# Retention and two feed-forward layers: layer 2's second product by seven products in two of its three pairs

## The chip, the cores and the metric

The kernel runs on one core of one Trainium2 chip. The metric is the device time in microseconds (us) of one execution: 847.47 us is the median of three runs of the kernel before (847.09 to 847.84). The engines named below are PE (TensorE, with its weight loads shown as PEld), DVE (VectorE), ACT (ScalarE), POOL (GpSimd) and SP (SyncE, which issues nearly all DMAs).

## The reference

```python
def _attn_ref(q, k, v):                      # batch 4, heads 8, sequence 576, head size 64
    scores = scale * np.matmul(q, k.transpose(0, 1, 3, 2))
    gamma = 1.0 - 2.0 ** (-5.0 - np.arange(H))
    Dmat = np.where(rel >= 0, gamma[:, None, None] ** rel[None, :, :], 0.0)
    return np.matmul(scores * Dmat[None], v)
...
x = attn_out.transpose(0, 2, 1, 3).reshape(2304, 512)
h = x @ moe_w_in;  g = np.maximum(0.01 * h, h);            x = g @ moe_w_out     # 512 -> 2048 -> 512
h = x @ moe2_w_in; g = h * (1.0 / (1.0 + np.exp(-h)));     return g @ moe2_w_out # 512 -> 2048 -> 512
```

The retention (attention without a softmax) feeds two feed-forward layers of the same size over 2304 tokens. Each layer has a first product (512 to 2048), a nonlinearity, and a second product (2048 to 512). Weights arrive as 64-bit floats and are turned into 32-bit floats on the chip.

## The kernel before

Every number that PE multiplies is split into a high and a low part (a `float32r` copy made by ACT in line 116, and the rest made by DVE in line 117). Each product is three matmuls: high by high, high by low, low by high (`PASSES`).

**The front** covers the first 1536 tokens of layer 1: three blocks of 512 tokens, 16 tiles of the hidden size (`f`) each, 48 *steps* in all (the loop of line 779). A step does `gemm1` (12 matmuls, `h<-xs,wi`), the nonlinearity and its split (`activate`), the splits of a weight tile (`split_wi`, `split_wo`), and `gemm2` of the step two before (12 matmuls, `acc<-g,wo`). The retention of the later tokens is laid between these matmuls at the times of `ATT_AT`. A layer 1 tile is *decoded* from 64-bit to 32-bit (`decode`, lines 371 to 393: two ACT and four DVE operations for 128x1024 numbers) in steps 0 to 13. The first 32 steps (`FIXED`) stand in a written order on every engine; the last 16 are ordered by a scheduler.

**The pairs.** Then come four *pairs* of 2x384 tokens: pair 0 is the rest of layer 1, pairs 1 to 3 are layer 2. A pair has eight *quads* (`k`), each two tiles of the hidden size. In a quad the first product is computed by seven products of sub-matrices in place of eight (`quad`; `sums_x` and `sums_w` make the sums of inputs and weights that this needs): 7x6 = 42 matmuls of 128x384 (`a` and `b`). Results are added in SBUF by DVE (line 594), go through the nonlinearity, and are split (`finish`) into `gh` and `gl`. The second product (`outputs`) is the plain one: 36 matmuls of 128x512 for a quad of pairs 1 to 3 (`outputs_y`), into six banks of PSUM that stay open over the pair (`acc0`, `acc1`, `att`). PE runs the second product of a quad between the seven products of the next one (`left`), which gives ACT and DVE time.

Layer 2's tiles are decoded in pairs 0 and 1 (`decoded`, line 866). Pair 1 also writes the split sums and the split second weights to DRAM (`kept`); pairs 2 and 3 fetch them (`fetch`, and line 527 in `weights_out`). PE and SP follow the written order in the pairs; ACT and DVE are ordered by the scheduler.

Of the kernel before, what the change touches and what calls it, by code (L numbers as in the profile page):

```python
# [26 lines left out]

FIXED = 2 * NF
TILE = 384
# [10 lines left out]

ATT_AT = (3.2, 8.4, 8.4, 13.8, 14, 22, 22, 29.8, 29.8, 36.5, 36.5, 43.1)
ATT = [(u, ATT_AT[2 * i], ATT_AT[2 * i + 1]) for i, u in enumerate(UNITS[2:])]
# [21 lines left out]
def retention_mlp_kernel(ctx: ExitStack, tc: tile.TileContext, qkva, qkvb, w1, w2, consts, out):  # L64
# [11 lines left out]
    x_p = pool("x", 1)  # L76
    s_p = pool("s", 29)
    hs_p = pool("hs", 2)
# [3 lines left out]
    st_p = pool("st", 4, stack=heads, side=right)  # L82
    acc_p = pool("acc", 1, PSUM)
    att_p = pool("att", 1, PSUM)
    ps_p = pool("ps", 2, PSUM)

    def slot(shape, dt, name):
        return s_p.tile(shape, dt, tag="s", name=name)

    cst = const.tile([128, NC + NP * CH], F32, name="cst")  # L90
# [256 lines left out]
    def load_w(layer, f, parts=(0, 1)):  # L347

        if (layer, f) not in w64:
            wraw[layer, f] = slot([128, 1024], F32, "wraw")  # L350
            w64[layer, f] = dec_p.tile([128, 1024, 2], I32, tag="w64", name="w64")
        src = (w1, w2)[layer][f].bitcast(I32)
        for i in parts:
            nc.sync.dma_start(out=w64[layer, f][:, i * 512:(i + 1) * 512].rearrange("p n t -> p (n t)"),
                              in_=src[:, i * 1024:(i + 1) * 1024])
        if len(parts) == 2:
            wdec.append((wraw[layer, f], w64[layer, f]))

    def half(f, i, by_act):

        c = slice(i * 512, (i + 1) * 512)
        return decode(wraw[0, f][:, c], w64[0, f][:, c], by_act)
# [44 lines left out]
    def split_x(layer, i, c, half=None, engine=nc.vector):  # L407
        p0, n = BLOCKS[i]
        if not half:
            xs[layer, i, c] = slot([128, 2, 512], F32R, "xs")  # L410
# [18 lines left out]
    def activate(layer, i, f):  # L429

        n = BLOCKS[i][1]
        h = hidden.pop((layer, i, f))
        hs = hs_p.tile([128, 512], F32, tag="hs", name="hs")
        g = slot([128, 2, 512], F32R, "g")
# [69 lines left out]

    dram = pool("scratch", 1, bass.MemoryType.DRAM)
    kept = {k: dram.tile([128, 22, 256], F32, tag=f"kept{k}", name="kept") for k in range(NF // 2)}
    PARTS = (("ha", 0, 3), ("la", 3, 3), ("hs", 6, 4), ("ls", 10, 4))

    def weights(p, k):

        t = {n: slot([128, m, 256], F32R, n) for n, _, m in PARTS}
        ha, la, hs, ls = t.values()
        for i, name in enumerate(("a11", "a12", "a22")):
            ww[p, k, name] = ha[:, i], la[:, i]
        for i in range(4):
            ww[p, k, f"s{i + 1}"] = hs[:, i], ls[:, i]
        return t

    def weights_out(p, k):

        for i in range(2):
            f = 2 * k + i
            wsp[p, f] = w = slot([128, 2, 512], F32R, "wo")
            there = kept[k][:, 14 + 4 * i:18 + 4 * i]
            here = w.bitcast(F32).rearrange("p a (b n) -> p (a b) n", b=2)
            if p > 1:
                nc.sync.dma_start(out=here, in_=there)
            else:
                yield from split(w[:, 0], w[:, 1], wraw[p, f][:, 512:], nc.vector)
                if p:  # L530
                    nc.sync.dma_start(out=there, in_=here)

# [6 lines left out]
    def sums_w(p, k):  # L539

        t = weights(p, k)
        ha, la, hs, ls = t.values()
        w, z = wraw[p, 2 * k], wraw[p, 2 * k + 1]
        a = w[:, :512].rearrange("p (c n) -> p c n", c=2)
        yield from split(ha[:, :2], la[:, :2], a, nc.vector)
        s = [hs_p.tile([128, 2, 256], F32, tag="hs", name="ws") for _ in range(2)]
        s1, s2, s3, s4 = (s[i // 2][:, i % 2] for i in range(4))
        yield nc.vector.tensor_tensor(out=s1, in0=z[:, :256], in1=z[:, 256:512], op=ALU.add)
        yield nc.vector.tensor_tensor(out=s2, in0=s1, in1=w[:, :256], op=ALU.subtract)
        yield from split(hs[:, :2], ls[:, :2], s[0], nc.vector)  # L550
        yield nc.vector.tensor_tensor(out=s3, in0=w[:, :256], in1=z[:, :256], op=ALU.subtract)
        yield nc.vector.tensor_tensor(out=s4, in0=w[:, 256:512], in1=s2, op=ALU.subtract)
        yield from split(hs[:, 2:], ls[:, 2:], s[1], nc.vector)
        yield from split(ha[:, 2], la[:, 2], z[:, 256:512], nc.vector)
# [12 lines left out]
    def finish(p, k, f, t, h):  # L567

        if (p, k, f) not in gp:
            gp[p, k, f] = [slot([128, 2 * TILE], F32R, n) for n in ("gh", "gl")]  # L570
        hi, lo = (x[:, t * TILE:(t + 1) * TILE] for x in gp[p, k, f])
# [14 lines left out]
    def quad(p, k):  # L586
# [30 lines left out]
        finish(p, k, 0, 1, c12)  # L617
        yield 4

    started = set()  # L620
# [55 lines left out]
    def decodes():  # L676
        while wdec:
            run(decode(*wdec.pop(0)))

# [97 lines left out]
    wo = iter(())  # L777
    second = ctx.enter_context(ExitStack())
    for t, (l, i, f) in enumerate(steps):
        first = t < FIXED  # L780
# [3 lines left out]
        if first:  # L784
# [17 lines left out]
            if t + 2 < NF:  # L802
                more_weights(min(NF, t + (4, 4, 5, 6)[min(t, 3)]))
            wi = split_wi(*steps[t + 2])
            if t == 0:
# [12 lines left out]
        else:  # L818
            run(a)
            run(wo)  # L820
            run(split_wo(l, i, f))
        if t >= LAG:
            for n, _ in enumerate(gemm2(*steps[t - LAG])):
# [9 lines left out]
        else:  # L833
            if t == len(steps) - 4:
# [3 lines left out]
                xt_p = pool("xt", 1, side=right, stack=second)  # L838
                dec_p = pool("dec", 2, side=right, stack=second)
                x0 = sums_x(0)  # L840
# [17 lines left out]
        if t == FIXED - 1:  # L858
            ordered.close()
    run(wo)  # L860
    run(x0)
    run(w0)
    later = ExitStack()
    later.enter_context(tc.manual_schedule(engines={mybir.EngineType.PE, mybir.EngineType.SP}))
    left = itertools.chain(*(gemm2(*st) for st in steps[-LAG:]))
    decoded = {0: (0, 1, 1, 1, 1, 1, 1, 0), 1: (0, 2, 2, 2, 2, 2, 0, 0)}
    x0 = iter(())
    for p in range(PAIRS):
        for k in range(NF // 2):
            after = (p, k + 1) if k + 1 < NF // 2 else (p + 1, 0)  # L870
            more = iter(())
            if after[0] < 2:
                more = sums_w(*after)
            elif after[0] < PAIRS:
                fetch(*after)
            coming = weights_out(p, k)
            if k == NF // 2 - 2 and p + 1 < PAIRS:
                x0 = sums_x(p + 1)
                coming = itertools.chain(coming, itertools.islice(x0, 3))
            if k == NF // 2 - 1:  # L880
                coming = itertools.chain(coming, itertools.islice(x0, 10))
            if k == 0 and p:
                coming = itertools.chain(x0, coming)
            todo = decoded.get(p, (0,) * NF)[k]
            for j, n in enumerate(quad(p, k)):
                for i in range(n):
                    next(left, None)
                    next(coming, None)
                    next(more, None)
                    next(more, None)  # L890
                next(coming, None)
                if j in (0, 2) and todo:
                    todo -= 1
                    run(decode(*wdec.pop(0), 512))
                    more_weights(nw + 1)
            run(left)
            run(more)
            run(coming)
            if (p, k) == (0, 0):
                more_weights(nw + 2)  # L900
            left = outputs(p, k)
    run(left)
    later.close()
# [62 lines left out]
```

## Time and profile before

| | |
|---|---|
| median of three runs | 847.47 us |
| profiled execution | 846.3 us, its span 844.6 us |
| PE busy | 828.4 us, 98% of the span |
| PE weight loads busy | 713.2 us, 84% |
| DVE busy | 486.3 us, 58% |
| ACT busy | 445.0 us, 53% |
| granted PE clock | 0.997 of full speed over the span |
| DMA | 127.94 MB, mean 151 GB/s |

A PE matmul is pipelined: its record lasts longer than the distance to the next one's start, so what a matmul costs is read from start to start, not from its duration. A window's PE busy time equal to its length means that PE never stood still in it. In the table of 40 slices each is some 21 us long.

### The profile page before, as it was taken

What the parts mean: (1) busy time and instruction counts of PE and PEld (TensorE: products, weight loads), DVE (VectorE), ACT (ScalarE), POOL (GpSimd) and SP (SyncE); (2) the same over time, 40 slices, a digit from 0 to 9 for tenths busy, and PEclk for the clock granted to TensorE, in tenths of its full rate; (3) what the DMA queues carried; (4) which work ended last, traced back from release to release, by engine and by line L of the source; (5) the groups of instructions that cost most, each with busy time, mean ns of one, the idle gap of its engine ahead of it and who ended that gap; (6) DMA issues with size and microseconds to landing.
All of it is one profiled execution on the core that took longest, in us unless ns stands there. A gap on an engine that the chain in (4) does not pass through costs nothing.

```text
span 844.6 us, 14065 instructions
## 1 busy us (share of the span) xinstructions
PE 828.4 (98%) x5736; PEld 713.2 (84%) x5736; DVE 486.3 (58%) x908; ACT 445.0 (53%) x783; POOL 17.7 (2%) x34
## 2 busy tenths in 40 slices
PE   8989999999999999999999999999999999999997
PEld 5677777777877778899999999999999999999996
DVE  6898975445544549776778788866322245322222
ACT  3777763343443336767667778865433345433332
POOL 5100000000000000000000000000000000000000
PEclk9999999999999999999999999999999999999999
DMA  9757511001111002021122489975794650885402
GB/s 337 288 190 252 203 69 67 31 37 66 67 67 66 2 2 100 1 99 51 52 99 88 165 315 344 347 274 187 290 329 143 220 188 1 295 328 171 154 0 75
DMA packets 38544, 127.94 MB, mean 151 GB/s; under 512 B 4304, under 2 KB 4432, under 8 KB 38480
## 3 DMA queue, kind: packets, MB, share of 16 engines
q1 hardware_dynamic: 38032, 126.26, 41.7%
q8 instruction: 45, 0.74, 0.4%
q10 hardware_dynamic: 448, 0.79, 0.3%
q14 instruction: 19, 0.16, 0.1%
HBM read 99.24 MB, written 27.79 MB: 150 GB/s over the span
## 4 chain that ended last, share of the span: by engine, by line
PE 90%; DVE 1%; ACT 0%; issue 0%
PE acc L138 35%; PE a L138 16%; PE h L138 13%; PE b L138 12%; PE att L138 10%; PE o L138 2%; PE r L138 2%; DVE st L282 0%; DVE pt L207 0%; DVE wraw L392 0%; DVE y L460 0%; DVE xs L117 0%; ACT hs L436 0%; DVE g L117 0%; DVE wi L117 0%
## 5 line engine op out<-in xcount | busy, mean ns | idle before, releaser
L138 PE MATMUL h<-xs,wi 128*128 128x512 f32 x576 | 147.2, 400 | 2.9 <-ACT wi L116 1.7
L138 PE MATMUL acc<-g,wo 128*128 128x512 f32 x576 | 142.5, 393 | 0.0
L594 DVE TENSOR_TENSOR X<-b,X 128x384 f32<-128x384 f32 x96 | 53.3, 556 | 144.3 <-ACT X L590 73.7
L138 PE MATMUL acc<-wo,gh 128*128 128x512 f32 x384 | 134.2, 391 | 0.0
L138 PEld LDWEIGHTS h<-xs,wi 128*128 128x128 f32 x576 | 106.0, 189 | 28.9 <-ACT wi L116 2.5
L138 PEld LDWEIGHTS acc<-g,wo 128*128 128x128 f32 x576 | 106.9, 188 | 22.6
L117 DVE TENSOR_TENSOR gl<-X,gh 128x384 fp32r<-128x384 f32 x128 | 70.9, 555 | 72.0 <-ACT gh L116 70.7
L590 ACT COPY X<-a 128x384 f32<-128x384 f32 x96 | 46.8, 488 | 116.0 <-PE a L138 115.1
L436 ACT ACTIVATE hs<-h 128x512 f32<-128x512 f32 x48 | 28.5, 595 | 120.0 <-PE h L138 120.0
L138 PEld LDWEIGHTS acc<-wo,gh 128*128 128x128 f32 x384 | 72.2, 188 | 13.3
L138 PE MATMUL acc<-wo,gl 128*128 128x512 f32 x192 | 75.2, 392 | 0.0
L117 DVE TENSOR_TENSOR g<-hs,g 128x512 fp32r<-128x512 f32 x48 | 33.1, 690 | 66.1 <-ACT g L116 66.1
L138 PE MATMUL att<-wo,gh 128*128 128x512 f32 x192 | 70.9, 390 | 0.0
L574 ACT ACTIVATE X<-X 128x384 f32<-128x384 f32 x72 | 38.1, 530 | 55.3 <-DVE X L594 55.3
L116 ACT CAST gh<-X 128x384 fp32r<-128x384 f32 x128 | 65.1, 514 | 3.4
L117 DVE TENSOR_TENSOR wo<-wraw,wo 128x512 fp32r<-128x512 f32 x80 | 54.9, 687 | 5.0 <-ACT wo L116 5.0
L116 ACT CAST wo<-wraw 128x512 fp32r<-128x512 f32 x80 | 49.3, 618 | 2.9 <-PE acc L138 2.9
L138 PE MATMUL acc<-gh,wo 128*128 128x512 f32 x128 | 48.6, 396 | 0.4 <-ACT gh L116 0.4
L382 ACT ACTIVATE w<-w,seven 128x512 uint16<-128x512 uint32 x30 | 44.0, 1466 | 0.4
L138 PE MATMUL a<-xh,hs 128*128 128x384 f32 x128 | 43.4, 339 | 0.0
L138 PE MATMUL b<-xh,hs 128*128 128x384 f32 x128 | 43.4, 339 | 0.0
L138 PE MATMUL a<-xh,ha 128*128 128x384 f32 x128 | 43.4, 339 | 0.0
(119 smaller groups left out, 1506.8 us busy)
## 6 DMA issues: line engine op xcount, KB each, us to landing
w<-in_w SPq DMA_DIRECT2D x64, 512.0 KB, 4.9
wo<-kept SPq DMA_DIRECT2D x32, 512.0 KB, 5.5
qkv<-in_qkvb SPq DMA_DIRECT2D x16, 672.0 KB, 5.1
kept<-wo SPq DMA_DIRECT2D x16, 512.0 KB, 6.6
hs<-kept SPq DMA_DIRECT2D x16, 512.0 KB, 4.8
ls<-kept SPq DMA_DIRECT2D x16, 512.0 KB, 5.9
ha<-kept SPq DMA_DIRECT2D x16, 384.0 KB, 4.4
la<-kept SPq DMA_DIRECT2D x16, 384.0 KB, 4.9
```

The source lines that it names most:

```text
L116: yield nc.scalar.copy(out=hi, in_=src)
L117: yield engine.tensor_tensor(out=lo, in0=src, in1=hi.bitcast(F32), op=ALU.subtract)
L138: return nc.tensor.matmul(out, lhsT, rhs, start=start, stop=stop, **kw)
L382: yield nc.scalar.activation(out=end[:, c], in_=lo[:, c].bitcast(U32), func=AF.Relu, scale=-2.0 ** -29, bias=seven)
L436: yield nc.scalar.activation(out=hs[:, :n], in_=h[:, :n], func=AF.Prelu, alpha=0.01)
L574: nc.scalar.activation(out=g, in_=h, func=AF.Silu)
L590: nc.scalar.copy(out=s, in_=a)
L594: nc.vector.tensor_tensor(out=s, in0=b, in1=s, op=ALU.add)
```

## The change

1. **Pairs 2 and 3.** The second product is computed by seven products as well. A pair is now in two phases: first all eight quads one after the other (`quad2`: its seven products use `a`, `b` and a third bank `d`, and after the Silu a result is kept whole, as 32-bit floats in `gu`), then the outputs (`outputs2`): seven products, each over eight `k`, three 128-token tiles and three passes, of 128x256 matmuls (504 in a pair). `operand` makes the sums and the splits of the left side (`ga`) ten units ahead on ACT and DVE; `fetch_out` brings the right side (`wb`), 512 KB for two `k`.
2. **Pair 1** makes the sums of layer 2's second weights for that (`sums_out`: four DVE subtractions of 128x256 and two splits for each `k`) and writes them to DRAM (`keptb`).
3. **Decoding of layer 2** moves from pairs 0 and 1 to sixteen of the steps 16 to 41 of the front (`DECODE_AT`). The decoded tiles of both layers are written to DRAM (`keep`) and fetched again where they are used: layer 1's in steps 12 to 47 and pair 0 four steps ahead, layer 2's in pairs 0 and 1 (`recall`).
4. The written order of the front covers 44 steps in place of 32, PE and SP stay in written order in the last four (`third`), the retention's times are a little earlier, `sums_w` works in place, and ten of the 29 slots of the shared pool become a pool of their own (`ring`).

```diff
-FIXED = 2 * NF
+FIXED = 3 * NF - 4
...
+def sums_out(p, k):
+    w, z = wsp[p, 2 * k], wsp[p, 2 * k + 1]
+    for name, x, i in (("b11", w, 0), ("b21", z, 0), ("b22", z, 1)):
+        nc.sync.dma_start(out=keptb[:, BS[name], k], in_=x.bitcast(F32)[:, :, i * 256:(i + 1) * 256])
...
+    yield nc.vector.tensor_tensor(out=b11, in0=b12, in1=b11, op=ALU.subtract)
+    yield nc.vector.tensor_tensor(out=b12, in0=b22, in1=b12, op=ALU.subtract)
+    yield from split(hi[:, 0], lo[:, 0], w.rearrange("p (e n) -> p e n", e=2), nc.vector)
...
+def quad2(p, k):
...
+    product(a, p, k, "a11", "b11", True)
+    c11 = copy(a)
+    product(b, p, k, "a12", "b21", True)
+    add(c11, b)
+    finish(p, k, 0, 0, c11)
+    product(a, p, k, "s2", "t2", False)
+    c12 = copy(a)
+    product(d, p, k, "s1", "t1", True)
+    c22 = copy(d)
+    product(a, p, k, "s3", "t3", False)
+    add(c22, a)
+    finish(p, k, 1, 1, c22)
+    product(d, p, k, "s4", "b22", False)
+    add(c12, d)
+    finish(p, k, 0, 1, c12)
+    product(a, p, k, "a22", "t4", False)
+    finish(p, k, 1, 0, a)
...
+SEVEN = (("a11", "b11"), ("a12", "b21"), ("s2", "t2"), ("s1", "t1"), ("s3", "t3"), ("s4", "b22"), ("a22", "t4"))
...
+def outputs2(p):
...
+    def mul(x, j, k, m, start, stop):
+        g, w = ga[p, j, k], wb[p, j, k // 2]
+        o = x[m // 2][:, m % 2 * 256:m % 2 * 256 + 256]
+        for i, (e, f) in enumerate(PASSES):
+            mm(o, g[:, e, m * 128:(m + 1) * 128], w[:, k % 2, f], ...)
...
+    for j in range(len(SEVEN)):
+        x = a if j in (0, 2, 4, 6) else pair(4, "d") if j == 3 else pair(2, "b")
...
+    nc.vector.tensor_copy(out=c21[:, 2], in_=a[1][:, :256])
+    store(p, 1, 0, c21, (2,))
...
+DECODE_AT = [16 + i * 27 // 16 for i in range(NF)]
...
-            elif t + 2 < NF:
-                d = decode(*wdec.pop(0), 512)
+            elif wdec and (t + 2 < NF or t in DECODE_AT):
+                done.append((t, wdec.pop(0)))
+                d = decode_tile(*done[-1][1], 512)
...
-    decoded = {0: (0, 1, 1, 1, 1, 1, 1, 0), 1: (0, 2, 2, 2, 2, 2, 0, 0)}
...
+            if p > 2 or p == 2 and k:
...
+                quad2(p, k)
```

What this does to the order, in three places. First PE in the second layer's later pairs. Before, matmuls of the second product (`acc<-wo,gh`, `acc<-wo,gl`: 128x512) stand between the products of the next quad (`a<-xh,hs`):

```order
L138 MATMUL acc<-wo,gl 128x512
L138 MATMUL acc<-wo,gh 128x512
L138 MATMUL a<-xh,hs 128x384
L138 MATMUL a<-xl,hs 128x384
L138 MATMUL a<-xh,ls 128x384
L138 MATMUL a<-xh,hs 128x384
L138 MATMUL a<-xl,hs 128x384
L138 MATMUL a<-xh,ls 128x384
L138 MATMUL acc<-wo,gh 128x512
```

Now, from the end of pair 2's last quad, the outputs are one stream of 128x256 matmuls, with the next pair's first product behind it:

```order
L144 MATMUL a<-xl,ha 128x384
L144 MATMUL a<-xh,la 128x384
L144 MATMUL a<-wb,ga 128x256 x72
L144 MATMUL b<-wb,ga 128x256 x72
L144 MATMUL a<-wb,ga 128x256 x72
L144 MATMUL d<-wb,ga 128x256 x72
L144 MATMUL a<-wb,ga 128x256 x72
L144 MATMUL b<-wb,ga 128x256 x72
L144 MATMUL a<-wb,ga 128x256 x72
L144 MATMUL a<-xh,ha 128x384
```

The 36 matmuls of a quad that stood between the products are gone from there; 504 half as wide stand together behind the eight quads.

Second DVE where the second block of the front ends (the last `xs` is the split of the third block's input, which its first matmuls read). Before:

```order
L117 TENSOR_TENSOR wo<-wraw,wo 128x512
L117 TENSOR_TENSOR g<-hs,g 128x512
L117 TENSOR_TENSOR wi<-wraw,wi 128x512
L117 TENSOR_TENSOR xs<-X,xs 128x512
L117 TENSOR_TENSOR g<-hs,g 128x512
```

Now, with the decode of a layer 2 tile (`wraw<-w`, lines 399 to 415):

```order
L331 TENSOR_TENSOR X<-o,cst 128x2x320
L399 TENSOR_SCALAR w<-w 128x512
L409 TENSOR_SCALAR wraw<-wraw 128x512
L412 TENSOR_SCALAR wraw<-wraw 128x512
L123 TENSOR_TENSOR wo<-wraw,wo 128x512
L415 SCALAR_TENSOR_TENSOR wraw<-w,wraw 128x1024
L123 TENSOR_TENSOR g<-hs,g 128x512
L185 TENSOR_TENSOR qkv<-qkv,cst 128x256
L123 TENSOR_TENSOR wi<-wraw,wi 128x512
L123 TENSOR_TENSOR xs<-X,xs 128x512
L213 TENSOR_TENSOR pt<-r,mask 128x384
```

Four operations of a decode now stand ahead of that split, of the retention's `pt` and of the splits between.

Third SP from the end of pair 1. Before, fetches of a quad and of its second weights, and the stores of pair 1's results (`out<-y`):

```order
L537 DMA ha<-kept 128x768
L537 DMA la<-kept 128x768
L537 DMA hs<-kept 128x1024
L537 DMA ls<-kept 128x1024
L527 DMA wo<-kept 128x1024 x2
L665 DMA out<-y 128x512 x6
L537 DMA ha<-kept 128x768
```

Now (there are seven groups of four `kept` fetches behind the stores, then the right sides of the outputs):

```order
L568 DMA keptb<-tl 128x4x256
L574 DMA ha<-kept 128x768
L574 DMA la<-kept 128x768
L574 DMA hs<-kept 128x1024
L574 DMA ls<-kept 128x1024
L856 DMA out<-y 128x512 x6
L574 DMA ha<-kept 128x768
...
L740 DMA wb<-keptb 128x1024 x18
L746 DMA out<-X 128x256 x3
L740 DMA wb<-keptb 128x1024 x10
```

The fetches of the second weights have left the quads; a quad fetches four pieces, and the outputs fetch 28 pieces of 512 KB.

## Rows read from the trace of the kernel before

**Rows 1.** The page: busy time; GB/s in 40 slices; the chain that ended last.

```profile
PE 828.4 (98%) x5736; PEld 713.2 (84%) x5736; DVE 486.3 (58%) x908; ACT 445.0 (53%) x783; POOL 17.7 (2%) x34
...
GB/s 337 288 190 252 203 69 67 31 37 66 67 67 66 2 2 100 1 99 51 52 99 88 165 315 344 347 274 187 290 329 143 220 188 1 295 328 171 154 0 75
...
PE 90%; DVE 1%; ACT 0%; issue 0%
```

**Rows 2.** Windows: engines' busy us (instructions), granted clock, DMA share, GB/s.

```profile
50.00:110.00 60.00, 57.61 (x590) 45.55 (x589) 52.99 (x112) 42.29 (x61) 1.32 (x4) 1.00 0.59 199
130.00:300.00 170.00, 170.00 (x1681) 135.25 (x1681) 84.98 (x170) 65.57 (x116) 0.69 (x7) 1.00 0.14 50
604.00:728.60 124.60, 124.60 (x625) 112.91 (x624) 42.14 (x70) 51.09 (x98) 0.00 (x0) 1.00 0.56 193
```

**Rows 3.** Timeline of PE in pair 0: start, duration, operation.

```profile
359.88 0.39 PE L138 MATMUL acc<-gl,wo 128*128 128x512 f32 x1
360.11 0.28 PE L138 MATMUL att<-gl,wo 128*128 128x256 f32 x1
360.23 0.39 PE L138 MATMUL acc<-gh,wo 128*128 128x512 f32 x1
...
361.61 0.34 PE L138 MATMUL a<-xh,ha 128*128 128x384 f32 x1
...
363.72 0.39 PE L138 MATMUL acc<-gh,wo 128*128 128x512 f32 x1
```

**Rows 4.** Timeline of the weight loads at the same place.

```profile
360.11 0.19 PEld L138 LDWEIGHTS acc<-gh,wo 128*128 128x128 f32 x1
360.23 0.19 PEld L138 LDWEIGHTS att<-gh,wo 128*128 128x128 f32 x1
```

**Rows 5.** Timeline of the last microseconds, all engines.

```profile
834.26 0.39 PE L138 MATMUL att<-wo,gl 128*128 128x512 f32 x1
...
838.57 0.39 PE L138 MATMUL att<-wo,gh 128*128 128x512 f32 x1
838.99 0.58 ACT L462 COPY y<-att 128x512 f32<-128x512 f32 x1 [0.77 <-PE att L138]
...
839.61 0.69 DVE L460 COPY y<-att 128x512 f32<-128x512 f32 x1 [0.67 <-ACT y L462]
```

**Rows 6.** Groups by shape, ACT: count, busy us, mean ns, idle before and releaser.

```profile
L116 ACT CAST gh<-X 128x384 fp32r<-128x384 f32 x128 | 65.1, 514 | 3.4
L590 ACT COPY X<-a 128x384 f32<-128x384 f32 x96 | 46.8, 488 | 116.0 <-PE a L138 115.1
L382 ACT ACTIVATE w<-w,seven 128x512 uint16<-128x512 uint32 x30 | 44.0, 1466 | 0.4
L574 ACT ACTIVATE X<-X 128x384 f32<-128x384 f32 x72 | 38.1, 530 | 55.3 <-DVE X L594 55.3
L371 ACT ACTIVATE wraw<-w 128x1024 f32<-128x1024 f32 x29 | 33.1, 1140 | 1.8 <-DMA w<-in_w 1.5 <-PE att L138 0.2
```

**Rows 7.** Groups by shape, DVE.

```profile
L594 DVE TENSOR_TENSOR X<-b,X 128x384 f32<-128x384 f32 x96 | 53.3, 556 | 144.3 <-ACT X L590 73.7 <-PE b L138 70.5
L392 DVE SCALAR_TENSOR_TENSOR wraw<-w,wraw 128x1024 int32<-128x1024 int32 x29 | 35.4, 1221 | 2.1 <-ACT w L382 2.0
L376 DVE TENSOR_SCALAR w<-w 128x512 uint16<-128x512 uint32 x34 | 26.5, 778 | 7.5 <-ACT wraw L371 7.3 <-issue 0.2
L386 DVE TENSOR_SCALAR wraw<-wraw 128x512 int32<-128x512 int32 x34 | 15.9, 468 | 0.0
L389 DVE TENSOR_SCALAR wraw<-wraw 128x512 int32<-128x512 int32 x30 | 12.6, 419 | 0.0
L551 DVE TENSOR_TENSOR ws<-wraw 128x256 f32<-128x256 f32 x16 | 6.7, 418 | 0.0
```

**Rows 8.** Timeline of PE where the first block of the front ends.

```profile
129.27 0.74 PE L138 MATMUL h<-xs,wi 128*128 128x512 f32 x2 [0.53 <-DVE xs L117]
```

**Rows 9.** DMA issues: operation, count, KB each, median us to landing.

```profile
hs<-kept SPq DMA_DIRECT2D x16, 512.0 KB, 4.8
```

More of the change, by code (lines that the diff above doesn't have):

```diff
@@ L356, in load_w, with keep, recall, decode_tile @@
         if len(parts) == 2:
-            wdec.append((wraw[layer, f], w64[layer, f]))
+            wdec.append((layer, f))
+    plain = [[dram.tile([128, 1024], F32, tag=f"plain{l}{f}", name="plain") for f in range(NF)] for l in range(2)]
+    def keep(layer, f):
+        nc.sync.dma_start(out=plain[layer][f], in_=wraw[layer, f])
+    def recall(layer, f):
+        wraw[layer, f] = slot([128, 1024], F32, "wraw")
+        nc.sync.dma_start(out=wraw[layer, f], in_=plain[layer][f])
+    def decode_tile(layer, f, by_act=0):
+        wraw[layer, f] = slot([128, 1024], F32, "wraw")
+        return decode(wraw[layer, f], w64[layer, f], by_act)
     def half(f, i, by_act):
+        if (0, f) not in wraw:
+            wraw[0, f] = slot([128, 1024], F32, "wraw")
         c = slice(i * 512, (i + 1) * 512)
@@ L778, in retention_mlp_kernel, with onward @@
     second = ctx.enter_context(ExitStack())
+    DECODE_AT = [16 + i * 27 // 16 for i in range(NF)]
+    done = []
+    def onward(t):
+        if NF <= t + 4 < len(steps):
+            recall(0, steps[t + 4][2])
+        if 0 <= t - len(steps) + 6 < 4:
+            recall(0, t - len(steps) + 6)
+        if t < 3:
+            keep(0, t)
+        while done and done[0][0] < t:
+            keep(*done.pop(0)[1])
+        if t >= NF - 2:
+            more_weights(NF + 3 + sum(x < t for x in DECODE_AT))
     for t, (l, i, f) in enumerate(steps):
@@ L862, in retention_mlp_kernel @@
     run(w0)
+    third.close()
     later = ExitStack()
@@ L875, in retention_mlp_kernel @@
                 fetch(*after)
-            coming = weights_out(p, k)
-            if k == NF // 2 - 2 and p + 1 < PAIRS:
+            if p < 2:
+                coming = weights_out(p, k)
+                q = p * NK + k + 2
+                if q < 2 * NK:
+                    for f in range(2):
+                        recall(q // NK, q % NK * 2 + f)
+            else:
+                units(p, k)
+            if k == NK - 2 and p < 2:
                 x0 = sums_x(p + 1)
                 coming = itertools.chain(coming, itertools.islice(x0, 3))
-            if k == NF // 2 - 1:
+            if k == NK - 1 and p < 2:
@@ L881, in retention_mlp_kernel @@
                 coming = itertools.chain(coming, itertools.islice(x0, 10))
-            if k == 0 and p:
+            if k == 0 and 0 < p < 3:
                 coming = itertools.chain(x0, coming)
[L884 to L887, printed above, removed]
-                    next(coming, None)
[L889 to L895, printed above, removed]
+            if p > 2 or p == 2 and k:
+                if k == NK - 1:
+                    for n in range(4):
+                        fetch_out(p, n)
+                quad2(p, k)
+            else:
+                for n in quad(p, k):
+                    for i in range(n):
+                        next(left, None)
+                        next(coming, None)
+                        next(more, None)
+                        next(more, None)
+                    next(coming, None)
@@ L898, in retention_mlp_kernel @@
             run(coming)
[L899 to L902, printed above, removed]
+            if p < 2:
+                left = outputs(p, k)
+            else:
+                operand(p, 0, k)
+            if (p, k) == (2, 0):
+                front.close()
+                bank_p = pool("bank", 1, PSUM)
+        if p > 1:
+            x0 = sums_x(p + 1) if p + 1 < PAIRS else iter(())
+            there, here = 4, NK
+            steps2 = outputs2(p)
+            for n in range(len(SEVEN) * NK):
+                while there < min(n // 2 + 10, len(SEVEN) * NK // 2):
+                    fetch_out(p, there)
+                    there += 1
+                while here < min(n + 10, len(SEVEN) * NK):
+                    operand(p, *divmod(here, NK))
+                    here += 1
+                if n >= 20:
+                    next(x0, None)
+                if n in (44,) and p + 1 < PAIRS:
+                    fetch(p + 1, 0)
+                if n < 6 * NK:
+                    next(steps2)
+            run(x0)
+            run(steps2)
     later.close()
```

191 lines of the change are left out of this document (151 added, 40 removed).

## The prediction

> **What bounds the kernel now.** I read the page's busy times first: PE is busy 98% of the span, the next engine 58%, and the chain that ended last lies on PE for 90% [rows 1]. Then the windows: over 170 us of the front and over 124.6 us, one whole pair, PE is busy for exactly the length of the window, at the full granted clock [rows 2]. So from 130 us on the time is the sum of PE's start-to-start slots plus a few waits, and DVE and ACT matter only where PE would come to wait for them. Only early in the front, 50 to 110 us, does PE stand still, 2.39 of 60 us, and there a weight tile is decoded in every step and DVE is 88% busy [rows 2].
>
> **Slots.** A matmul's record is longer than its share of PE, so I take distances between starts. A stream of 128x512: from 834.26 to 838.57 there are 19 steps, 0.227 us each [rows 5]. A stream of 128x384: from 361.61 to 363.72 there are 12, 0.176 each [rows 3]. The 128x256 shape of the new code is in the trace only in turns with 128x512: 360.11 to 360.23, 0.12, while the pair of them from 359.88 to 360.23 takes 0.35 [rows 3], so 0.35 - 0.227 = 0.123 for the small one. A straight line through 0.176 and 0.227 gives 0.125 at 256 columns. Five such pairs lie between 359.88 and 361.61, 0.346 each, by which it is 0.119. I take 0.1185, from the longest stretch; bounds 0.113 (0.346 less 0.23, the distance after the long one at 359.88, less rounding) and 0.125. As a check on the method, a pair of before by these slots is 8 x 42 x 0.1755 + 8 x 36 x 0.2275 = 59.0 + 65.5 = 124.5 us; the window that holds one has 124.6 [rows 2].
>
> **Part 1, the second product of pairs 2 and 3.** It removes 288 matmuls of 128x512 from each pair, 65.5 us, and adds 504 of 128x256, 504 x 0.1185 = 59.7. The first product keeps its 336 matmuls in another order. That is -5.8 us a pair and **-11.6 us** for both (-5.0 at 0.125, -17.1 at 0.113). Changes between shapes inside a quad fall away; the check above leaves at most 0.3 us a pair for them: -0.3 in all.
>
> Do the engines beside PE keep up? In a quad of before PE has 15.5 us; now 42 x 0.175 = 7.35. For it ACT does three copies of 0.488, four Silus of 0.53 and one split of 0.514: 4.1 us; DVE three additions of 0.556 and the three operations of `operand`, 3.3 us [rows 6, 7]. The three banks are each needed again at earliest one product (1.05 us) after the product that filled them, and a copy of 0.488 or an addition of 0.556 fits, with some 0.2 us to spare after its start latency. Where the previous pair's results are still being evacuated (0.58 on ACT and 0.69 on DVE each [rows 5]), a quad can come late: I put 0.5 us a pair, bounds 0 and 2, **+1.0**. In the outputs DVE has 56 splits of 0.556, some 16 more sums of that size, the additions and, in pair 2, the next pair's input sums: about 54 of 60 us. That is a tight row, but `operand` runs ten units of 1.07 us ahead; I cost it at nothing, bounds 0 and 2.
>
> Fetches: a quad now needs 1.8 MB each 7.35 us, 250 GB/s; four issues (two of 384 KB, two of 512 KB, a landing of the larger some 4.8 us [rows 9]). By the order on SP most are issued two to four quads ahead, since nothing but slots holds them. Only the first quads behind output stores are close, and I put 0.3 us for each of two: **+0.6**, bounds 0 and 2.
>
> **Part 2, the sums in pair 1.** Per quad DVE gets four subtractions of 0.418 [rows 7] and two splits at about 0.69, ACT two at about 0.58, as the copies of 128x512 [rows 5]; the two decodes that stood in the same quads cost DVE 0.778 + 0.468 + 0.419 + 1.221 = 2.89 and ACT 1.140 + 1.466 = 2.61 each [rows 6, 7]. Both engines have less to do than before. Nothing, with PE's full quads of 15.5 us as the cover.
>
> **Part 3, the decode in the front.** Sixteen decodes bring DVE 46 us and ACT 42 us more between about 127 and 300 us. In the window 130 to 300 DVE was busy 85 of 170 us and ACT 66 [rows 2]; they become about 77% and 63%. PE's matmul count does not change, so this is free as long as no split that a matmul waits for comes late. The one place where the trace shows such a wait is a block's end: 0.53 us at 129.27, on the split of the next block's input [rows 8]. That one has no new decode ahead of it. At the end of the second block it has: the four operations of a decode now stand ahead of `xs` on DVE, start to start some 2.4 us (their sum of 2.89 less the overlap of one with the next). Queued behind `xs` there is the retention's `pt`, which PE also reads. The window before the next matmul of the new block takes up most of it; I put a third of 2.4, **+0.8**, bounds 0 and 2.4. The upper bound for the whole stage is a rival below.
>
> **Parts 3 and 4, stores and fetches of decoded tiles.** 512 KB each way, beside a queue that is busy 14% in this window [rows 2]. In steps 0 to 13 the stores stand ahead of the next weights on SP, where the queue already moves 199 GB/s [rows 2]; a landing comes later by a store of the same size or two: **+0.3**, bounds 0 and 2. In pair 1 the bytes stay about the same: the new stores and fetches replace the loads of 64-bit weights.
>
> **The tail.** Before, the last matmul starts at 838.57, ACT copies one bank from 838.99, then DVE the other until 840.30, and the last store follows [rows 5]. Now one DVE copy of half the width, 0.42 by the same-sized row [rows 7], starts when the ACT copy did and ends at about 839.4: **-0.9**, bounds -1.2 and 0.
>
> **Sum.** -11.6 - 0.3 - 0.9 + 1.0 + 0.6 + 0.8 + 0.3 = -10.1. The profiled execution took 846.3 us (844.6 its span); the median of the runs is 1.2 longer. On the profiled one the sum gives 836.2, on the median 837.4. I say **837.0**.
>
> **Two rules beside the rows.** Loads of weights: one of 128x128 is recorded at 0.19 us, and its neighbours start 0.12 apart, so records overlap [rows 4]. The Trainium skill, "TensorE: Matmul & The Clock Gate", section "LDWEIGHTS (loading the stationary operand)", puts a load of 128 columns at about 107 ns; by that figure, an estimate, 504 loads take 53.9 us a pair, and the loads would not set the pace. The trace's 0.12 between loads is near it but the 0.19 is not.
> Another section there, "Back-to-back issue gap", gives a sustained 131 ns for streams of 512 columns and 81 for 128. The trace disagrees at 512, where it has 0.227, so its figure is not used; its other formula, columns over 2.4 plus 2.5 ns, makes 109 ns for 256 columns and the sum -10.6 a pair in place of -5.8. The same formula gives 216 at 512 where the row has 227, so I keep the rows.
>
> **Rivals.**
> *Slower: the small matmuls are paced by their weight load.* Each 128x256 matmul needs a load of its own, recorded at 0.19 us, longer than its slot [rows 4]. In the trace a long matmul follows each short one, so a late load could be made good there; in a stream of 504 it could not. At 0.188 a slot the outputs of a pair take 94.8 us in place of 65.5, +29.3, and with both pairs the kernel takes 847.5 + 58.6 - 1 = 905. It turns slower from 65.5 / 504 = 0.130 us a slot. Against it: the load for the matmul at 360.23 began at 360.11, 0.12 before, right when the short one did, and the one for 360.45 at 360.23; loads do overlap. A stream of 384 columns also runs at 0.176, under the load's 0.19, without falling behind [rows 3]. Chance 0.06.
> *The front pays.* If DVE at 77% made PE wait as at 88% in 50 to 110 us, that is 4.0% of 170 us, +6.8 [rows 2], and the sum is about 843.5. For it: in-order DVE with a decode ahead of splits, as there. Against it: ten of the 26 steps have no decode, and PE's idle time at 50% is not small but nought, so there is slack to use up first. Chance 0.10.
> *Fetch-bound quads.* If a quad's weights only began to land when a slot of the last one came free, each quad would take about 9.6 us (four landings of some 4.8, two at a time [rows 9]), in place of 7.35, +2.2 in 14 quads, 31 us, on 837 some 868. For it: a quad asks at a higher rate than before. Against it: 250 GB/s is under the 344 and 347 of two slices [rows 1], and the order has no dependence that close. Chance 0.05.
> *The waits eat it.* With every wait at its upper bound (2 + 2 + 2 + 2.4 + 2 = 10.4 in place of 2.7) and the tail at nothing the kernel takes 847.5 - 11.9 + 10.4 = 846.0, no change; with the slot at 0.125 as well, 852.6. Chance 0.04.
>
> **From these to the numbers.** The forecast holds 0.75, with its own range 831 (slot at 0.113, waits at half) to 844 (0.125 with the waits as put). About 0.2% (1.7 us) is what a measurement of this kernel can tell from no change. Faster by more: the forecast 0.75, and 0.08 of the front rival: 0.83. Within it: 0.02 of the front rival and 0.03 of the last one: 0.05. Slower: 0.06 + 0.05 of the two slow rivals and 0.01 of the last: 0.12. The range 830 to 846 takes in the front rival and leaves out the slower ones, 0.12, and a little at either end.
>
> **What would show it.** PE's starts in the outputs of pair 2: 0.1185 apart confirms part 1; 0.13 or more refutes it. PE's idle time in 130 to 300 us: under 1 us confirms part 3. Gaps on PE before a first product of a quad, with a DMA as releaser, would be the fetches; with ACT or DVE as releaser, the banks. The end 1 us or less nearer to the last matmul is the tail. The forecast is wrong if the outputs of a pair last longer than 62 us, or if PE's idle time from 130 us to the end passes 6 us.

## The result and the profile after

The changed kernel takes 836.26 us (median of four runs, 835.6 to 837.36), the kernel before 847.62; the ratio is 0.9868 with a 95% interval of 0.9851 to 0.9885. That is 11.4 us less, where 10.5 were forecast. Two more sets of runs of the same kernel, told below, gave 0.985 and 0.9861.

The page of the changed kernel: busy time by engine, GB/s in 40 slices, the chain that ended last.

```profile
PE 820.1 (98%) x6168; PEld 725.8 (87%) x6168; DVE 565.9 (68%) x1082; ACT 471.1 (56%) x855; POOL 18.0 (2%) x34
...
GB/s 331 308 308 315 280 344 317 259 305 269 315 297 281 199 142 101 50 58 95 51 89 207 182 317 293 323 240 259 192 407 218 272 271 133 328 325 190 281 231 58
...
PE 87%; DMA 2%; DVE 1%; ACT 1%; issue 0%; DVEq 0%
```

Beside [rows 1] PE has lost 8.3 us of work and is still busy 98%; DVE has gained 80 us and the queue moves over 250 GB/s through the first third. For the first time a DMA stands in the chain, with 2%. The windows of the changed kernel (columns as in [rows 2]): 50 to 110 us, steps 16 to 47, and the outputs of pair 2.

```profile
50.00:110.00 60.00, 57.39 (x589) 45.32 (x589) 53.20 (x112) 42.32 (x61) 1.67 (x4) 1.00 0.88 297
127.14:331.39 204.25, 204.25 (x1969) 162.67 (x1968) 155.55 (x294) 120.49 (x183) 0.79 (x8) 1.00 0.70 250
650.80:710.80 60.00, 60.00 (x502) 60.00 (x501) 46.42 (x87) 29.90 (x61) 0.00 (x0) 1.00 0.67 229
```

DVE is busy 76% of steps 16 to 47 and PE never stands still there; 502 matmuls in 60.00 us make 0.1195 a slot, and from the first start of the outputs to the 504th, 650.78 to 711.12, it is 0.120.

The stages, as starts of PE's matmuls in the two profiled executions (us of the span). Quad (2,1) is quad 1 of pair 2, counted from 0: the first in the new order.

| | before | after | difference of the stage |
|---|---|---|---|
| first matmul of the front (`h`) | 22.89 | 23.20 | +0.31 |
| step 16 | 126.18 | 127.14 | +0.65 |
| first quad | 328.74 | 331.39 | +1.69 |
| quad (2,1) | 596.83 | 597.09 | -2.39 |
| last matmul | 838.57 | 832.08 | -6.75 |
| end of the span | 844.58 | 835.63 | -2.46 |

The sum is -8.95; the profiled execution is the slowest of the four (837.36), so the median shows more. The stages before and after the first quad go together, since the scheduler of before had put some of the front's second products there: -0.70 for both.

Where PE waited in pairs 2 and 3 of the changed kernel (timeline of PE, the waits with their releaser):

```profile
601.70 0.44 PE L144 MATMUL a<-xh,hs 128*128 128x384 f32 x1 [0.24 <-ACT X L673]
...
605.75 0.44 PE L144 MATMUL a<-xh,la 128*128 128x384 f32 x1 [0.28 <-DMA la<-kept]
...
608.30 0.44 PE L144 MATMUL a<-xh,ls 128*128 128x384 f32 x1 [0.18 <-DMA ls<-kept]
...
722.00 0.44 PE L144 MATMUL a<-xh,ls 128*128 128x384 f32 x1 [0.61 <-DMA ls<-kept]
```

The first is in quad (2,1), which takes 7.87 us; the next two in (2,2), 8.36; the last in (3,1), 8.39. The last quads of both pairs, (2,7) and (3,7), take 7.90 and 7.75, with waits of 0.1 us and less in the records. A quad without a wait takes 7.39. From start to start a wait is longer than its note says, since the record of the matmul before it reaches into it.

The end, all engines:

```profile
829.93 0.42 DVE L806 COPY y<-a 128x256 f32<-128x256 f32 x1 [5.50 <-ACT y L805]
832.40 0.42 DVE L808 COPY y<-a 128x256 f32<-128x256 f32 x1 [2.04 <-PE a L144]
```

Against [rows 5], one copy stands behind the last matmul (832.08). It ends at 832.82, and the span 2.8 us later; before, it was 4.3 from the last copy's end (840.30) to 844.58. The stores issued behind the last copy (KB, us from issue to landing), before and after:

```profile
out<-y ACTq DMA_DIRECT2D x1, 256.0 KB, 3.2
```

```profile
out<-y SPq DMA_DIRECT2D x1, 128.0 KB, 1.7
```

In both kernels one store is left. Before, it is of 256 KB and two others, issued at 839.60 and 839.63, are still under way; now it is of 128 KB.

### The profile page after: what moved, and what is told of

The parts are those of the page before. It is cut to its first block, busy times and chain, and to the rows that moved or that the text cites. A ratio compares the mean times of both kernels' runs of the same rounds, so it can differ in the third digit from the quotient of the medians.

```text
span 835.6 us, 15630 instructions
## 1 busy us (share of the span) xinstructions
PE 820.1 (98%) x6168; PEld 725.8 (87%) x6168; DVE 565.9 (68%) x1082; ACT 471.1 (56%) x855; POOL 18.0 (2%) x34
## 4 chain that ended last, share of the span: by engine, by line
PE 87%; DMA 2%; DVE 1%; ACT 1%; issue 0%; DVEq 0%
PE acc L144 25%; PE a L144 23%; PE h L144 14%; PE b L144 12%; PE d L144 5%; PE att L144 5%; PE o L144 2%; DMA ls<-kept 2%; PE r L144 2%; DVE wo L123 0%; ACT X L673 0%; DVE ls L123 0%; DVE st L288 0%; ACT wo L122 0%; DVE wraw L415 0%
## 5 line engine op out<-in xcount | busy, mean ns | idle before, releaser
L144 PE MATMUL a<-wb,ga 128*128 128x256 f32 x576 | 70.4, 283 | 0.0
L144 PEld LDWEIGHTS a<-wb,ga 128*128 128x128 f32 x576 | 69.8, 192 | 0.0
L631 DVE TENSOR_TENSOR X<-b,X 128x384 f32<-128x384 f32 x51 | 28.4, 556 | 59.1 <-ACT X L627 52.9
L719 ACT CAST ga<-gq 128x384 fp32r<-128x384 f32 x72 | 36.1, 513 | 21.9 <-PE a L144 10.4
L715 DVE TENSOR_TENSOR ga<-gq,ga 128x384 fp32r<-128x384 f32 x72 | 38.7, 556 | 13.8 <-ACT ga L719 13.7
L415 DVE SCALAR_TENSOR_TENSOR wraw<-w,wraw 128x1024 int32<-128x1024 int32 (+1 forms) x35 | 39.7, 1133 | 11.9 <-ACT w L405 11.6
L123 DVE TENSOR_TENSOR gl<-X,gh 128x384 fp32r<-128x384 f32 x64 | 35.5, 555 | 18.0 <-ACT gh L122 18.0
L144 PE MATMUL acc<-wo,gh 128*128 128x512 f32 x128 | 44.8, 391 | 0.0
L144 PE MATMUL a<-xh,ls 128*128 128x384 f32 x128 | 43.5, 340 | 0.8 <-DMA ls<-kept 0.8
L144 PE MATMUL a<-xh,la 128*128 128x384 f32 x128 | 43.3, 338 | 0.3 <-DMA la<-kept 0.3
```

What stands on the lines that cost most here:

```text
L123: yield engine.tensor_tensor(out=lo, in0=src, in1=hi.bitcast(F32), op=ALU.subtract)
L144: return nc.tensor.matmul(out, lhsT, rhs, start=start, stop=stop, **kw)
L415: yield nc.vector.scalar_tensor_tensor(out=wi, in0=hi, scalar=-0x7FFFFFF9, in1=wi, op0=ALU.bitwise_and, op1=ALU.bitwise_xor)
L631: nc.vector.tensor_tensor(out=s, in0=b, in1=s, op=ALU.add)
L715: order(nc.vector.tensor_tensor(out=out, in0=a, in1=b, op=op))
L719: nc.scalar.copy(out=t[:, 0], in_=x)
```

## The experiments

All changes are against the changed kernel. The start of the front moves by itself (see below), so traces are compared from the front's first matmul on. Each set of runs has one trace.

**Halves: is the slot set by columns or by the weight load?**

```diff
-                mm(o, g[:, e, m * 128:(m + 1) * 128], w[:, k % 2, f], ...)
+                for s in range(2):
+                    mm(o[:, s * 128:(s + 1) * 128], g[:, e, m * 128:(m + 1) * 128], w[:, k % 2, f, s * 128:(s + 1) * 128], ...)
```

Expected: 

> Each 128x256 matmul of the outputs of pairs 2 and 3 is done as two of 128x128, each with its own weight load (1008 a pair in place of 504); nothing else changes. If the number of columns sets the slot, the straight line through the slots of 384 and 512 columns in the trace of before (0.176, 0.227) and the measured 0.120 at 256 gives about 0.07: 1008 x 0.07 = 70.6 in place of 60.4 a pair, about +20 us in all, 856. If a weight load sets the pace and a load every 0.12 us is all there is, the slot stays 0.12: 1008 x 0.12 = 121, +60.5 a pair, +121 in all, 957.

Measured (one run): 938.72 us. The window of pair 2's outputs, and its groups on PE (count, busy, mean ns):

```profile
649.20:761.20 112.00, 112.00 (x1005) 112.00 (x1004) 50.24 (x87) 31.47 (x61) 0.00 (x0) 1.00 0.38 124
```

```profile
L144 PE MATMUL a<-wb,ga 128*128 128x128 f32 x572 | 64.5, 274 | 0.0
L144 PE MATMUL b<-wb,ga 128*128 128x128 f32 x288 | 32.5, 274 | 0.0
```

The outputs run from 649.16 to 761.55: 0.1116 a matmul, where the line through the wider shapes gives about 0.07. Half the columns save 7% of the slot, and the time is nearer to the 957 us of a slot that stays than to the 856 of one set by columns. So a load with its matmul costs PE about 0.11 us, however short the matmul, and the 256-column slot of 0.120 lies just above that floor. The slower rival has a floor of this kind; its price (0.188, the recorded load) was not the true one, and at 0.1116 it does not decide at 256 columns. That the floor is the load's own was not tried, as no run uses a load for two matmuls. For it speaks that a fixed price of each matmul is far smaller: in the changed kernel's trace 40 matmuls of the retention, each with a load too, but of 64x64, lie within 0.81 us.

```profile
125.60 0.81 PE L144 MATMUL r<-qkv 64*64 64x64 f32 x40
```

The Trainium skill, "TensorE: Matmul & The Clock Gate", section "LDWEIGHTS (loading the stationary operand)", puts a load of 128 columns at about 107 ns, which is near the 0.1116 us.

**Plain: the front and pairs 0 and 1 alone.** Pairs 2 and 3 keep the second product of before, so pair 1 makes no sums for them either.

```diff
+                nc.sync.dma_start(out=here, in_=there)
...
-        if p > 1:
-            nc.scalar.activation(out=gu[p, 2 * k + f][...], in_=h, func=AF.Silu)
-            return
...
-            if p > 2 or p == 2 and k:
...
-                quad2(p, k)
-            else:
-                for n in quad(p, k):
+            for n in quad(p, k):
```

Expected: 

> The changed front and pairs 0 and 1 (decode of layer 2 in steps 16 to 41, stores and fetches of decoded tiles, the changed order) alone: pairs 2 and 3 keep the second product of before, 36 matmuls of 128x512 a quad, with its split weights stored in pair 1. Theory: all of the gain comes from the second product and the tail, the front costs nothing; the traces have quad 17 start at 596.83 before and 597.09 after, so this kernel takes as long as before: 847.6 to 848.5 us. Rival: the front pays for the decode, as in 50 to 110 us of before (4.0% of 170 us, +6.8): 852 to 855. Second rival: the front gains by the new order: 845 to 846.

Measured: 846.79 us (11 runs, 846.02 to 848.31) beside 847.8; ratio 0.999 (0.9981 to 0.9998). Its quad (2,1):

```profile
596.63 0.34 PE L144 MATMUL a<-xh,ha 128*128 128x384 f32 x1
```

It starts 573.62 us behind the front's first matmul, where it was 573.94 before. The decode of layer 2 in the front, 46 us more of DVE there, and the stores and fetches of decoded tiles cost nothing; pair 1's sums are not in this kernel, but from the first quad to quad (2,1) it takes 265.65 us and the changed kernel 265.70. The median lies 1.0 us (0.2 to 1.6) under that of before, and 0.8 under the expected range; the traces show 0.4 of it. So of the 11.4 us about 10 come from the second product and the tail.

**Light and dense: how much room has the front?** Light leaves out all of layer 2's decode but its first ACT operation (`light` is set for layer 2 alone); dense puts one in each of the steps 16 to 31.

```diff
+        if light:
+            yield from (None, None, None)
+            return
```

```diff
-    DECODE_AT = [16 + i * 27 // 16 for i in range(NF)]
+    DECODE_AT = [16 + i for i in range(NF)]
```

Expected of light: 

> The changed kernel, with only the first ACT operation of each decode of layer 2 (it leaves out the other ACT operation and the four DVE operations, so layer 2's weights are not the right ones; the number of matmuls, stores and fetches is the same). Theory: the decodes cost PE nothing where they stand, so from step 16 (start at 127.14) to the first quad (331.39) it takes as long as the changed kernel within 0.4 us: 203.9 to 204.3. Rival: they hold PE up by more than the trace's waits show, and it takes 1 us less or more.

Expected of dense: 

> The changed kernel with the sixteen decodes of layer 2 in steps 16 to 31, one in each. Theory: DVE goes from some 77% to about 90% busy in these steps, and PE still waits little since the splits that a matmul reads come two steps ahead: from step 16 to the first quad less than 1.5 us longer than in the changed kernel (204.3 us). Rival: it is the share of DVE that decides, as in 50 to 110 us of before (88% busy, 4.0% of the time lost): +3.5 us or more. PE's waits then lie at products of the retention and at blocks' ends.

Measured, one execution each. Light: 204.02 us from step 16 to the first quad, in place of 204.25; whole time 835.81. Dense: 204.82, so 0.57 more; 836.58. In the other traces with the changed front this stage lies between 204.19 and 204.27. Windows of dense, steps 16 to 31, and its one wait on PE in steps 16 to 47:

```profile
127.80:232.80 105.00, 105.00 (x1105) 83.13 (x1104) 88.73 (x173) 71.49 (x98) 1.36 (x5) 1.00 0.95 356
```

```profile
236.77 0.73 PE L144 MATMUL h<-xs,wi 128*128 128x512 f32 x2 [0.31 <-DVE xs L123]
```

What light leaves out costs PE 0.23 us where it stands. At 85% DVE and 95% DMA PE still does not wait inside the steps, only once at the block's end, on the very split that the prediction named. So up to 85% the share of DVE does not decide: what PE reads comes early enough. What else makes PE stand still in 50 to 110 us was not tried.

**Tail: the last product in the order of the others.**

```diff
-        for m in range(3):
-            for k in range(NK):
-                mul(a, 6, k, m, False, True)
...
+        for k in range(NK):
+            for m in range(3):
+                mul(a, 6, k, m, False, True)
...
+        nc.scalar.copy(out=c21[:, 0], in_=a[0][:, :256])
+        nc.vector.tensor_copy(out=c21[:, 1], in_=a[0][:, 256:])
+        store(p, 1, 0, c21, range(2))
```

Expected: 

> The changed kernel, with the last of the seven products ordered by k as the other six (in place of by the 128-token tile), so that all three of its results are copied and stored after the last matmul. Theory: from the last matmul's start to the end of the span it is 6.0 us before and 3.55 after, because only one copy of 128x256 and one store of 128 KB are left; with three copies (ACT and DVE at the same bank, one behind the other) and four stores behind it the end comes 1.2 to 2.5 us later in pair 3, and pair 2's copies are hidden by the next pair: 837.5 to 838.8. Rival: the tail is shorter for another reason (the store's landing, 1.7 us for a small store whatever stands before it), and the time changes by less than 0.6 us: 836.3 to 836.9.

Measured: 839.71 us (838.47 to 840.53), 3.5 over the changed kernel's first set. Its trace has only 1.8 us of that at the end, so it ran once more beside the changed kernel:

> The kernel with the last product ordered by k again. Theory: its trace has 5.38 us from the last matmul's start to the end in place of 3.55; 1.8 us longer than the changed kernel, and the rest of the 3.4 us by which its median was longer was the start of the front (first matmul at 24.25 us in place of 22.88 to 23.4). Rival: the order of the last product costs more than the tail shows, and the medians differ by 3 us again.

838.43 us (838.0 to 839.66) beside 835.74. The end of the second trace:

```profile
830.98 0.37 ACT L804 COPY y<-a 128x256 f32<-128x256 f32 x1 [9.93 <-PE a L144]
831.33 0.42 DVE L807 COPY y<-a 128x256 f32<-128x256 f32 x1 [7.97 <-PE a L144]
831.38 2.23 SPq L746 DMA_DIRECT2D out<-y  x4
831.67 0.41 DVE L805 COPY y<-a 128x256 f32<-128x256 f32 x1
```

Two DVE copies stand one behind the other, and from the end of the last (832.08) to that of the span (836.38) it is 4.3 us. That is the length of before by another way: SP issues four stores one behind the other, from 831.38 to 833.60, and each lands in about 1.9 us. From the last matmul it is 5.37 us in place of 3.55. That is 1.8 of the 2.7 us. The whole is nearer to the rival's 3 us than to the theory's 1.8, and the start of the front is not the rest: here the first matmul comes at 22.88. In both traces of this kernel quad (3,1) waits for its fetch (8.25 and 8.52 us), in the changed kernel's later two hardly (7.40 and 7.62). Whether the order of the last product brings that about was not settled.

**Early: fetches ahead of stores.**

```diff
+                if after == (2, 2):
+                    flush(1)
...
-                if n in (44,) and p + 1 < PAIRS:
-                    fetch(p + 1, 0)
+                if n in (44, 48, 52) and p + 1 < PAIRS:
+                    fetch(p + 1, (n - 44) // 4)
```

`flush(1)` issues pair 1's stores, which are kept back until there.

Expected: 

> The changed kernel, with fetches moved ahead of output stores on SP: pair 1's out<-y stores stand behind the fetch of quad (2,2), and the fetches of (3,1) and (3,2) stand ahead of the stores of pair 2's last product. Theory: the two quads that took 8.35 and 8.40 us in place of 7.39 (starts at 604.96 and 718.63) waited for fetches that came late because SP stood behind the stores; without it both take 7.4 to 7.5 and the kernel is about 1.9 us faster, 834.3. Rival: they waited because the queue was full of later fetches (landings of 9 us in place of 4 to 6), and the order does not matter: 836.3, no change, with waits of the same size at the same or the next quads.

Measured: 835.93 us (835.08 to 836.12). Queue of SP in the changed kernel, and then in this one:

```profile
597.90 1.06 SPq L856 DMA_DIRECT2D out<-y  x2
599.38 0.33 SPq L574 DMA_DIRECT2D ha<-kept  x1
599.77 0.47 SPq L574 DMA_DIRECT2D la<-kept  x1
```

```profile
591.42 0.32 SPq L574 DMA_DIRECT2D ls<-kept  x1
593.40 5.90 SPq L850 DMA_DIRECT2D out<-y  x6
599.39 0.41 SPq L574 DMA_DIRECT2D ha<-kept  x1
```

Quad (2,2)'s `la` left SP at 599.77 for a matmul that should have started at 605.3; in the early kernel all four pieces leave by 591.4. The two quads take 7.37 and 7.39, and from quad (2,1) to the last matmul it is 233.21 us in place of 234.99: -1.8, about what the theory has. Later its quad (3,6) takes 7.67, for a cause not found. The median, though, moves by 0.3 only, against 836.26, as the rival has it. The next runs explain why.

**Again: the changed kernel unaltered.**

Expected: 

> The changed kernel once more, unaltered, on the chip of the next ones. The traces so far have the first matmul of the front between 22.88 and 24.25 us, whatever the kernel, so medians of four runs may be off by half a microsecond: 835.6 to 837.4.

Measured: 835.24 us (835.09 to 835.37), ratio 0.985 (0.9834 to 0.9866). That is below the expected range. In its trace (2,2) takes 7.56 and (3,1) 7.40: the fetches arrived nearly in time by themselves. It has 233.23 from quad (2,1) to the last matmul, as the early kernel has. So the late fetches are a close race that only some executions lose, and the executions of this set lose little by it. For the rival it speaks that the queue is full then: on the changed kernel's page a landing of these pieces takes 8.9 us, where [rows 9] has 4.8.

```profile
hs<-kept SPq DMA_DIRECT2D x16, 512.0 KB, 8.9
ls<-kept SPq DMA_DIRECT2D x16, 512.0 KB, 8.9
```

Whether the early order takes the wait away is not shown: the three traces with it (early and the two of best, below) have none at these two quads, but of the eight without it light, dense and halves have none either.

**Best: the operand of pair 2's first unit behind the second quad.** On top of the early kernel.

```diff
-            else:
-                operand(p, 0, k)
+            elif (p, k) == (2, 1):
+                operand(p, 0, 0)
+                operand(p, 0, 1)
+            elif (p, k) != (2, 0):
+                operand(p, 0, k)
```

Expected: 

> The kernel with early fetches, and in pair 2 the operand of the first output unit (a split and two sums on DVE) stands behind the second quad's products, not ahead of them. Theory: in quad (2,1) PE waits 0.39 us because the addition of the second product stands behind these three DVE operations (1.7 us), the Silu behind the addition, and the copy of the bank that PE wants behind the Silu on ACT; so this quad goes from 7.86 to 7.4, -0.5 us against the early kernel, -2.1 us against the changed one (from the front's first matmul to the end), about 834.3. Rival: the evacuations of pair 1's results, which stand ahead of both, are what makes it late: 7.86 stays, and the time is that of the early kernel, 835.

Measured: 836.45 us (834.44 to 837.92). DVE in quad (2,1) of the changed kernel, and then of this one:

```profile
598.51 0.55 DVE L715 TENSOR_TENSOR ga<-X,ga 128x384 fp32r<-128x384 f32 x1
599.10 1.15 DVE L715 TENSOR_TENSOR X<-X 128x384 f32<-128x384 f32 x2
600.17 0.55 DVE L677 TENSOR_TENSOR X<-b,X 128x384 f32<-128x384 f32 x1
```

```profile
597.37 0.69 DVE L483 COPY y<-att 128x512 f32<-128x512 f32 x1 [0.67 <-ACT y L485]
598.93 0.56 DVE L677 TENSOR_TENSOR X<-b,X 128x384 f32<-128x384 f32 x1 [0.86 <-PE b L144]
```

The evacuations are ahead in both; with the three operand operations gone the addition waits for PE, not the other way, and the quad takes 7.37 in place of 7.87. From quad (2,1) to the last matmul it is 232.62. The medians did not show it, so both ran again on one chip.

> The kernel with early fetches and the later operand again, beside the changed kernel on the same chip, since four times of it lay between 834.4 and 837.9. Theory: from the front's first matmul to the end it takes 809.8 us, 0.8 less than the changed kernel at its best and 2.6 less than in its first profile; its median is 0.8 to 2 us under that of the changed kernel. Rival: the start of the front, which differs from execution to execution by over 1 us, hides this, and the medians lie within 0.8 us.

> The changed kernel, unaltered, on the same chip: 835.2 to 836.3 us.

Best: 835.11 us (834.7 to 836.93), the changed kernel: 835.74 (835.11 to 838.23); ratios to before 0.9852 (0.9836 to 0.9868) and 0.9861 (0.9838 to 0.9884). The medians differ by 0.63 us, within the noise and under the theory's 0.8. From quad (2,1) to the last matmul the traces have 232.61 and 233.28. So 0.6 to 0.7 us is in both pairs of traces, and the times do not show it.

From the front's first matmul to the end it is 811.79 us in place of the 809.8 expected, and longer than the changed kernel's 811.05. The loss is in the front, which takes 105.70 us to step 16 where the first trace of best has 103.77. The granted clock of TensorE fell there. The windows of the second trace:

```profile
52.00:56.00 4.00, 1.57 (x18) 1.38 (x19) 3.79 (x13) 2.52 (x4) 0.34 (x1) 0.69 0.90 282
56.00:60.00 4.00, 4.00 (x11) 3.04 (x10) 2.96 (x5) 2.21 (x3) 0.00 (x0) 0.50 0.65 135
```

Twelve matmuls, with the wait ahead of them, in the second trace, and then the same twelve in the first:

```profile
54.43 0.71 PE L144 MATMUL o<-pt,qkv 64*64 64x64 f32 x16 [2.91 <-DVE sa L288]
55.07 5.44 PE L144 MATMUL h<-xs,wi 128*128 128x512 f32 x12
```

```profile
53.93 3.01 PE L144 MATMUL h<-xs,wi 128*128 128x512 f32 x12
```

They take 5.44 us in place of 3.01 at half the clock (0.50, the level of 1.2 GHz). It fell while PE waited 2.91 us for the retention's `sa`, until 54.43.

## Why the prediction was right

**The slot.** Forecast 0.1185, measured 0.120; 504 slots take 60.5 us in place of 59.7, where 288 took 65.5 [rows 2, 5]. That is 1.5 us short for both pairs. The check on the method held too: 7.39 a quad against 7.35. Neither sign of a wrong forecast came: the outputs stayed under 62 us, and PE's idle time from 130 us to the end is 2.3 us, not 6.

**What hides behind PE.** That DVE at 77% would not hold PE up was right (76%, no wait shown). The 0.8 us for the end of the second block was too much: dense has the wait there at 0.31 us with a decode in every step, and the changed kernel has none that the trace notes. The 0.53 us of [rows 8] fell away too; that was not forecast. Light puts the cost of the decodes at 0.23. DVE's work in the outputs was put at 54 of 60 us and is 46.4. The upper rival for the front (+6.8) is refuted by plain and dense.

**Quads.** 1.0 us for ACT and DVE: quad (2,1) lost 0.48, and the last quads of the pairs 0.51 and 0.36. The prediction put the blame on evacuations; best shows that in quad (2,1) the operand's three operations were it. Why the last quads lose was not tried. Fetches: 0.6 forecast, 2.0 in the profiled execution (0.97 and 1.00), 0.2 in each of the next two. The first quads behind output stores are late, as was said, and only those.

**The tail** was the term most out: -0.9 forecast, -2.46 measured. The copy was sized rightly (0.42, one in place of two: 0.99 us less). What failed is "the last store follows", taken as equal in length: it lands 1.7 us after its issue in place of 3.2, and from the copy to the end it is 2.8 us in place of 4.3. Whether the half size or the empty queue shortens it was not separated.

**The early front** was put at +0.3 and took +0.65 from the first matmul to step 16. The mechanism is the one forecast, a later landing, and 0.47 of it stands in one place, where ACT waits for the 64-bit weights and PE for the split made from them. Before, and then in the changed kernel:

```profile
38.05 1.14 ACT L371 ACTIVATE wraw<-w 128x1024 f32<-128x1024 f32 x1 [1.53 <-DMA w<-in_w]
43.01 1.22 PE L138 MATMUL h<-xs,wi 128*128 128x512 f32 x3 [1.49 <-ACT wi L116]
```

```profile
38.79 1.14 ACT L394 ACTIVATE wraw<-w 128x1024 f32<-128x1024 f32 x1 [1.95 <-DMA w<-in_w]
43.79 1.52 PE L144 MATMUL h<-xs,wi 128*128 128x512 f32 x3 [1.97 <-ACT wi L122]
```

Between 50 and 110 us, where the queue moves 297 GB/s in place of 199, PE is idle 0.2 us more.

**The sum.** In the profiled execution the span is 1.15 us longer than the sum had it. Pairs 2 and 3 are 3.55 over (-6.75 for -10.3: the slot 1.5, the fetches 1.4, the rest small), the tail is 1.56 under, and the front with pairs 0 and 1 0.84 under (+0.26, its start among it, for +1.1). No term was out by more than 1.6 us, but that 837.0 lies so near is in part luck: the errors cancel, and the late fetches that the first trace has cost hardly anything in the next two, where from the front's first matmul to the end it takes 11.0 and 10.6 us less than before.

## What to carry to other kernels

A shape that the trace shows only between other shapes can be priced by the distance between starts, as long as the floor beneath it is known: halve it once and see. Work moved under a bound engine is nearly free (0.23 us here) when what the bound engine reads is ready a step ahead, here with up to 85% of the engine that gets it; the places to look at are block ends and phase ends, where one in-order engine still holds something else. At the end of a kernel leave one small store behind the last matmul, not several; here that is worth 1.8 us. And count how many executions lie behind a difference: two traces of one kernel differed by as much as most of the effects here.

## What the runs showed of the hardware

- A stream of 128x128 weight loads, each with a matmul of 128 columns in `float32r`, runs at 0.1116 us a pair, though a load is recorded at 0.192 and its records overlap; 256, 384 and 512 columns run at 0.120, 0.176 and 0.227. So 128 columns cost 93% of what 256 cost.
- The records of the loads cover a window wholly (60.00 of 60.00 us at 256 columns, 112.00 of 112.00 at 128), so their share does not tell the two apart.
- The front's first matmul starts between 22.88 and 24.25 us, with the same code: in the trace that began latest, of the tail kernel, matmuls of the retention waited at 9.37 and 10.72 us for the first loads, in that of "again" (22.88) not.

```profile
9.37 0.71 PE L144 MATMUL r<-qkvk 64*128 64x128 f32 x8 [0.27 <-DMA qkvk<-in_qkva]
10.72 0.71 PE L144 MATMUL r<-qkvk 64*128 64x128 f32 x8 [0.64 <-DMA qkvk<-in_qkva]
```

That is up to 1.4 us. Two more differences between executions are seen in traces, and each is as large: the late fetches (up to 2.0 us) and the granted clock.

- In most traces the granted clock is at half for 3.4 us between 44 and 50 us. In the second trace of best it is so for 6.8 us from 53.5 on, and the front takes 1.9 us longer than in the first. The runs of one set of four spread over 0.3 to 3.5 us, more than most of the effects here. How much of a given run's time is due to each of the three is not shown; counting a trace from the first matmul on takes out the first only.
